# A gated linear attention with a mixture of experts: the state's part of the outputs on four array quarters, a new order on TensorE, decays in three buffers with a budget, and choices for six chunks at a time

## The chip, the cores and the metric

The kernel runs on one core of a Trainium2 chip. The core has a matrix engine (TensorE, PE in the profile; its weight loads are PEld), a vector engine (VectorE, DVE), a scalar engine (ScalarE, ACT), GpSimd (POOL), and SyncE (SP), which issues most of the transfers (DMA). Each engine runs its own list of instructions in order and waits at semaphores for the others. SBUF is the working memory of 128 partitions. PSUM is the memory that TensorE writes to; it has eight banks of 512 float32 numbers per partition.

The metric is the time of one execution on the device in microseconds (us), as the median of several runs.

## What is computed

The reference runs a gated linear attention and gives its result to a mixture of 16 experts in 4 groups:

```python
def _attn_ref(q, k, v, alpha):            # (B, H, S, D) = (4, 8, 768, 48)
    for t in range(S):
        state = alpha[:, :, t, :, None] * state + einsum('bhd,bhe->bhde', k[:, :, t], v[:, :, t])
        y[:, :, t] = einsum('bhd,bhde->bhe', q[:, :, t], state)

def _moe_ref(x, w_group, w_expert, w1, w2):   # x: 3072 tokens of 384
    g_idx = argmax(x @ w_group)               # one of 4 groups, with its softmax weight
    e_idx = argmax(x @ w_expert[g_idx])       # one of 4 experts of the group, with its weight
    out = g_w * e_w * (relu(x @ w1[g, e]) @ w2[g, e])     # 384 -> 1024 -> 384
```

All data are float32. Every token goes to one expert.

## The kernel before

**The attention loop.** The sequence of each of the 4 batches is cut into 6 chunks of 128 tokens. The loop `for n in range(LAST)` (L559) goes over all 24 chunks. The 8 heads are held as 4 pairs (HP = 4). Of a pair, one head lies in partitions 0 to 47 and the other in 64 to 111, so that TensorE can work on both halves of its rows at once. For each chunk there is

- `decayed` (L251): for each pair, two scans on VectorE (L271, L279) that multiply up the decays alpha, backwards and forwards, with a small reciprocal between them (L277), and two products on GpSimd that scale the keys (kp, L274) and the queries (qp, L281). This is done for a *unit* of chunks at once: units have 1, 2 and 3 chunks in batch 0, and 3 and 3 in the others, nine units in all.
- `scores` (L285): for each head, keys times queries on TensorE (L293), 8 matmuls of 128 columns.
- `masked` (L297): the scores go from PSUM to SBUF through an ACT copy (L305) and a GpSimd select that zeroes the future (L306). For some halves VectorE multiplies with a mask instead (L302).
- `turned_keys` (L311): 4 transposes of the keys on TensorE (L318) and an ACT copy (L319).
- `gains` (L322): keys times values, what the chunk adds to the state (L330). `grown` (L336) adds it to the old state on VectorE (L338), and `scaled` (L341) multiplies by the chunk's decay in four ACT instructions (L346). At the end of a batch there is no state to carry, and gains, transposes and state's part are left out.
- `from_before` (L350): the state's part of the chunk's output, state times queries, 8 small products of 48 rows and 48 columns (L358).
- `outputs` (L363): the chunk's own part, values times masked scores (L370), added in PSUM onto the state's part. Each pair's two heads go to the two halves of the output partitions.
- `copied` (L375): an ACT copy of the output to SBUF, named yt.
- `to_rows` (L380): TensorE turns yt into rows by token and multiplies by the group and expert weights in one go (L389). ACT copies the rows to xr (L400), and VectorE sums up the logits (L394).

In a step, TensorE runs: turned keys of n, state's part of n, gains of n, outputs of n, scores of n+1, then to_rows of n.

**The choice.** `choose` (L404) finds group and expert for some chunks at a time with small VectorE instructions (L418 to L435, the picks) and then their weights (L442 to L452). `send` (L455) counts tokens per expert with two matmuls (L462, L463), and VectorE makes a place for every token (L469 to L481). `scatter` writes a chunk's rows to their places in DRAM (slots_d) with an indirect DMA on GpSimd (L490). The choice is made for three chunks at a time (in the last batch three, two and one). Its pieces wait in a queue, `gates`, and the decays' pieces in another, `decays`; `take` (L511) issues a fixed number of them at fixed points of a step.

**What sets the order.** The program is written in the order in which each engine runs it (`manual_schedule`). Only the waits between engines are derived. A pool of PSUM tiles, `bank()`, has seven buffers, one bank each; an eighth bank holds constants.

**Loads.** SP issues the loads of a unit's data (L242, four transfers per unit), the values (L248), a fill of the slots with blanks (L614), and then the expert weights (L178, L180). The first three units are loaded into the buffers that will later hold expert weights, others into seven buffers of their own.

**The experts.** After the loop, 17 jobs run: the first expert's first 128 tokens from the first three batches (`early_rows`, read by L497 once chunk 17 has been scattered), its other tokens, and then one job for each of the other 15 experts, the fullest first. A job has 48 weight tiles, in `hidden` (L639) and `result` (L655). Results go out through VectorE and an indirect DMA on GpSimd (L693). The order of the experts, the rows of the second job (L820) and the weights of the third wait for the last chunk's scatter.

Of the kernel before, what the change touches and what calls it, by code (L numbers as in the profile page):

```python
# [16 lines left out]
ALU = mybir.AluOpType  # L17
# [17 lines left out]
def gla_then_hierarchical_moe(  # L35
# [68 lines left out]
    pp = ctx.enter_context(tc.tile_pool(name="psum", bufs=7, space=PSUM))  # L104
    dp = ctx.enter_context(tc.tile_pool(name="dram", bufs=1, space=DRAM))

    def bank():
        return pp.tile([P, 512], F32, name="bank")
# [55 lines left out]

    early_rows = cp.tile([P, EARLY // 32, QW], F32, name="early_rows")

    weights = {}

    def busy(k, w=P):

        z = bank()
        for _ in range(k):
            nc.tensor.matmul(z[:, 0:w], lhsT=ident, rhs=ident[:, 0:w], start=True, stop=True)
# [29 lines left out]

    with ExitStack() as gla:
        buf = gla.enter_context(tc.tile_pool(name="buf", bufs=1))
        inp = gla.enter_context(tc.tile_pool(name="inp", bufs=7))
        prep = gla.enter_context(tc.tile_pool(name="prep", bufs=2))
        work = gla.enter_context(tc.tile_pool(name="work", bufs=2))
# [6 lines left out]
        NU = len(units)  # L215
        where = {b * NC + c0 + c: (u, c) for u, (b, c0, k) in enumerate(units) for c in range(k)}
# [3 lines left out]
        homes = {}  # L220
        spare, width = [], 0
        for u in range(3):
            w = units[u][2] * (2 * P + A1) + 1
            for p in range(HP):
                if not spare or width + w > DC * F:
                    k = len(spare)
                    spare.append(wp.tile([P, DC, F], F32, name="w1").rearrange("p c f -> p (c f)")
                                 if k % 2 == 0 else
                                 wp.tile([P, FC, DM], F32, name="w2").rearrange("p c f -> p (c f)"))
                    width = 0  # L230
                homes[u, p] = spare[-1][:, width:width + w]
                width += w

        def load(u):
            b, c0, k = units[u]
            at = sum(k_ * (2 * P + A1) + 1 for b_, c_, k_ in units if b_ == b and c_ < c0)
            w = k * (2 * P + A1) + 1
            for p in range(HP):
                t = homes.pop((u, p), None)
                if t is None:  # L240
                    t = inp.tile([P, UC * (2 * P + A1) + 1], F32, name="qka")
                nc.sync.dma_start(out=t[:, 0:w], in_=qka_d[b, p, :, at:at + w])  # L242
                loaded[u, p] = t[0:R]

        def load_v(b, c0=0, c1=NC):
            if c0 == 0:
                vs[b] = prep.tile([P, NC, DM], F32, name="v")
            nc.sync.dma_start(out=vs[b][:, c0:c1].rearrange("p c e -> p (c e)"),  # L248
                                in_=v_d[b, :, c0 * DM:c1 * DM])

        def decayed(u, p):  # L251
# [16 lines left out]
            cq = prep.tile([R, UC, A1], F32, name="cq")[:, 0:k_, :]  # L268
# [14 lines left out]
            return [(1.0, back), (1.2, forth)]  # L283

        def scores(n):  # L285
            u, c = where[n]
            qp, kp, _ = ready[u]
            z = [bank() for _ in heads]
            for p in range(HP):
                if p and n < 2:  # L290
                    busy(1, 64)
                for i, r in enumerate(heads):
                    nc.tensor.matmul(z[i][:, p * P:(p + 1) * P], lhsT=kp[r, p, c, :],  # L293
                                     rhs=qp[r, p, c, :], start=True, stop=True)
            return [t.rearrange("p (h i) -> p h i", h=HP) for t in z]

        def masked(z, on_vector=0):  # L297

            sm = work.tile([P, 2, HP, P], F32, name="sm")
            for i in range(2):  # L300
                if i < on_vector:
                    nc.vector.tensor_tensor(out=sm[:, i], in0=z[i], in1=causal[:, None, :]  # L302
                                            .to_broadcast([P, HP, P]), op=ALU.mult)
                    continue
                nc.scalar.copy(out=sm[:, i], in_=z[i])  # L305
# [5 lines left out]
        def turned_keys(n):  # L311

# [3 lines left out]
            kt = work.tile([P, HP * R], F32, name="kt")  # L316
            for p in range(HP):
                nc.tensor.transpose(zt[:, p * R:(p + 1) * R], kp[:, p, c, :], ident[0:R, 0:R])  # L318
            nc.scalar.copy(out=kt, in_=zt[:, 0:HP * R])  # L319
# [3 lines left out]

# [12 lines left out]
        def grown(n, st, add):  # L336

# [4 lines left out]

# [6 lines left out]

        def from_before(n, st):  # L350
# [3 lines left out]
            z = bank()  # L354
            for p in range(HP):
                for i, r in enumerate(heads):
                    o = slice(64 * i, 64 if i == 0 else R)
                    nc.tensor.matmul(z[o, p * P:(p + 1) * P],  # L358
                                     lhsT=st[r, p, 0:o.stop - o.start], rhs=qp[r, p, c, :],
                                     start=(p == 0), stop=False, skip_group_check=True)  # L360
            return z

        def outputs(n, sm, z):  # L363

            b, bc = divmod(n, NC)
            for p in range(HP):
                for i in range(2):
                    h = 2 * p + i
                    o = slice(64 * i, 64 if i == 0 else R)
                    nc.tensor.matmul(z[o, p * P:(p + 1) * P],  # L370
                                     lhsT=vs[b][:, bc, h * D:h * D + o.stop - o.start],
                                     rhs=sm[:, i, p, :], start=(p == 0 and bc == 0), stop=True,
                                     skip_group_check=True)

        def copied(z):  # L375
            yt = work.tile([R, HP, P], F32, name="yt")
            nc.scalar.copy(out=yt.rearrange("r p s -> r (p s)"), in_=z[0:R, :])  # L377
            return yt

        def to_rows(n, yt):  # L380

# [3 lines left out]
            x, lg = xs[b]  # L385
# [5 lines left out]
            z = z[:, 0:HP * W].rearrange("s (p w) -> s p w", p=HP)  # L391

            def logits():
                nc.vector.tensor_reduce(out=lg[:, bc, :],  # L394
                                        in_=z[:, :, D2:W].rearrange("s p w -> s w p"),
                                        axis=AX.X, op=ALU.add)

            if n + 1 == LAST:
                logits()
# [577 lines left out]
```

## Time and profile before

| | us |
|---|---|
| median of three runs | 430.98 |
| lowest and highest | 430.56, 432.88 |
| the profiled execution | 431.07 |
| its span, first to last instruction | 429.3 |
| first scores on TensorE (L293) | from 6.41 |
| last to_rows of the loop (L389) | 148.55 to 149.70 |
| first expert matmul (L639) | from 151.33 |
| last expert matmul done | 405.6 |
| busy in the span: TensorE, VectorE, ACT, GpSimd | 396.3, 163.8, 124.4, 213.4 |
| busy from 11 to 150: TensorE, VectorE, ACT, GpSimd | 127.3, 98.1, 75.9, 99.6 |
| mean clock granted to TensorE | 0.962 |

A line of a timeline has the start, the duration of the group, the engine, the line of the source, the operation, what it writes and reads, the shapes, how many instructions are merged into the line, and in brackets how long the engine sat idle before it and what ended that. A float32 matmul is recorded as two instructions, so 8 matmuls make x16. The ends of matmuls are modelled, and consecutive groups overlap by some 0.07 us; the time of a group is therefore read from its start to the next one's start.

### The profile page before, as it was taken

How to read it: one execution, taken by the hardware profiler on the slowest of the kernel's cores; microseconds unless marked ns; L12 is line 12 of the kernel's file. 1: busy time of each engine (PE TensorE's matmuls, PEld its weight loads, DVE VectorE, ACT ScalarE, POOL GpSimd, SP SyncE). 2: the span in 40 equal slices, each digit the busy share in tenths (PEclk: the TensorE clock that was granted, in tenths of full speed). 3: DMA queues.
4: the chain of work that ended last, by engine and by line, in shares of the span. 5: the costliest groups of instructions: out<-in, count | busy, mean ns of one | idle time of the engine just before them, and what ended most of it. 6: DMA issues, size and time to landing. Idle time of an engine off the chain costs nothing.

```text
span 429.3 us, 8796 instructions
## 1 busy us (share of the span) xinstructions
PE 396.3 (92%) x3352; PEld 376.9 (88%) x3352; DVE 163.8 (38%) x457; ACT 124.4 (29%) x304; POOL 213.4 (50%) x275
## 2 busy tenths in 40 slices
PE   4998989989889898799999999999999999999991
PEld 3887878778778688799999999999999999999990
DVE  6767668588784471202074120220220222022100
ACT  1466546266465421011121111111111121121110
POOL 7787548597794562210532623623623532452351
PEclk9999889699999989889999999999999999999997
DMA  7998994889111336895865966766876876856000
GB/s 258 394 404 305 359 395 136 263 308 351 53 40 58 96 111 227 223 332 212 274 192 186 279 226 193 245 256 200 241 266 202 271 247 221 300 187 276 34 24 26
DMA packets 32220, 95.23 MB, mean 222 GB/s; under 512 B 18111, under 2 KB 18902, under 8 KB 27696
## 3 DMA queue, kind: packets, MB, share of 16 engines
q1 hardware_dynamic: 27360, 85.10, 58.1%
q0 software_dynamic: 4816, 9.55, 6.8%
q8 instruction: 27, 0.44, 0.4%
q14 instruction: 17, 0.14, 0.1%
HBM read 79.47 MB, written 15.56 MB: 221 GB/s over the span
## 4 chain that ended last, share of the span: by engine, by line
PE 55%; issue 3%; POOL 2%; DMA 1%; DVE 0%; SPq 0%; POOLq 0%; ACT 0%; DVEq 0%; ACTq 0%
PE bank L639 28%; PE bank L655 27%; POOL out_dram L693 1%; DMA slots_d<-xr,place 1%; DMA xq<-slots_d 0%; POOL out_dram L678 0%; POOL yT L628 0%; SPq L820 0%; DVE yq L686 0%; DVE yq L689 0%; POOLq L885 0%; ACT yT L657 0%; DVE dst_q L710 0%; DVE xt_e L701 0%; POOLq L678 0%
## 5 line engine op out<-in xcount | busy, mean ns | idle before, releaser
L693 POOL DMA_INDIRECT out_dram<-yq,dst_q x99 | 96.4, 974 | 158.8 <-DVE yq L689 120.1
L639 PE MATMUL bank<-xt_e,w 128*128 128x128 f32 (+16 forms) x816 | 136.8, 329 | 6.0 <-issue 4.1
L639 PEld LDWEIGHTS bank<-xt_e,w 128*128 128x128 f32 x816 | 133.7, 196 | 6.9 <-issue 6.5
L655 PE MATMUL bank<-hT,w 128*128 128x128 f32 (+16 forms) x816 | 131.8, 321 | 0.0
L655 PEld LDWEIGHTS bank<-hT,w 128*128 128x128 f32 x816 | 129.6, 190 | 0.0
L641 ACT ACTIVATE hT<-bank 128x256 f32<-128x256 f32 (+16 forms) x68 | 32.6, 479 | 108.1 <-PE bank L639 105.7
L710 DVE CAST dst_q<-xq 128x7 int32<-128x7 f32 (+2 forms) x16 | 2.7, 166 | 160.0 <-DMA out_dram<-yq,dst_q 160.0
L657 ACT COPY yT<-bank 128x192 f32<-128x192 f32 (+32 forms) x34 | 13.3, 391 | 113.8 <-PE bank L655 113.8
L306 POOL TENSOR_SCALAR_AFFINE_SELECT sm<-sm 128x512 f32<-128x512 f32 x43 | 26.4, 635 | 27.8 <-ACT sm L305 27.8
L293 PE MATMUL bank<-qp,kp 48*128 48x128 f32 x384 | 31.6, 300 | 6.7 <-POOL qp L281 6.7
L293 PEld LDWEIGHTS bank<-qp,kp 48*128 48x128 f32 x384 | 25.2, 196 | 11.2 <-POOL qp L281 6.9
L370 PE MATMUL bank<-sm,v 128*48 128x128 f32 (+1 forms) x384 | 31.4, 297 | 0.4
L389 PE MATMUL bank<-wr,yt 112*128 112x116 f32 x192 | 28.3, 292 | 1.4 <-ACT yt L377 1.1
L490 POOL DMA_INDIRECT slots_d<-xr,place x24 | 24.2, 1010 | 9.9 <-DVE starts L418 4.7
L305 ACT COPY sm<-bank 128x512 f32<-128x512 f32 x43 | 23.3, 588 | 15.6 <-PE bank L293 14.0
L389 PEld LDWEIGHTS bank<-wr,yt 112*128 112x128 f32 x192 | 24.0, 197 | 3.9 <-ACT yt L377 2.8
L370 PEld LDWEIGHTS bank<-sm,v 128*48 128x48 f32 (+1 forms) x384 | 24.8, 142 | 2.6 <-POOL sm L306 1.2
L358 PE MATMUL bank<-qp,state 48*48 48x128 f32 (+1 forms) x320 | 24.9, 302 | 0.0
L279 DVE TENSOR_TENSOR_SCAN cq<-qka,starts 112x387 f32<-112x387 f32 x24 | 23.0, 959 | 2.5
L346 ACT ACTIVATE state<-gained,rev 112x48 f32<-112x48 f32 x64 | 16.2, 323 | 26.1 <-DVE gained L338 21.9
L281 POOL TENSOR_TENSOR qp<-qka,cq 112x384 f32<-112x384 f32 x24 | 21.9, 914 | 2.6 <-DVE cq L279 2.4
L274 POOL TENSOR_TENSOR kp<-qka,rev 112x384 f32<-112x384 f32 x24 | 22.4, 934 | 1.1 <-DVE rev L271 0.9
(122 smaller groups left out, 300.7 us busy)
## 6 DMA issues: line engine op xcount, KB each, us to landing
w<-in_w_dram SPq DMA_DIRECT2D x32, 1536.0 KB, 7.0
qka<-in_qka_dram SPq DMA_DIRECT2D x24, 578.0 KB, 11.0
slots_d<-blank SPq DMA_DIRECT2D x1, 5488.0 KB, 22.9
v<-in_v_dram SPq DMA_DIRECT2D x3, 1152.0 KB, 14.2
xq<-slots_d SPq DMA_DIRECT2D x32, 85.8 KB, 7.3
w<-in_qka_dram SPq DMA_DIRECT2D x4, 578.0 KB, 9.5
xq<-slots_d SPq DMA_DIRECT2D x28, 73.5 KB, 6.1
out_dram<-yq,dst_q POOLq DMA_INDIRECT x99, 5.8
```

The source lines that it names most:

```text
L279: nc.vector.tensor_tensor_scan(out=flat(cq), data0=a[:, 0:W], data1=st, initial=1.0, op0=ALU.mult, op1=ALU.min)
L293: nc.tensor.matmul(z[i][:, p * P:(p + 1) * P], lhsT=kp[r, p, c, :], rhs=qp[r, p, c, :], start=True, stop=True)
L305: nc.scalar.copy(out=sm[:, i], in_=z[i])
L306: nc.gpsimd.affine_select(out=sm[:, i], in_=sm[:, i], pattern=[[0, HP], [1, P]], compare_op=ALU.is_ge, fill=0.0, base=0, channel_multiplie ...
L358: nc.tensor.matmul(z[o, p * P:(p + 1) * P], lhsT=st[r, p, 0:o.stop - o.start], rhs=qp[r, p, c, :], start=(p == 0), stop=False, skip_group_ ...
L370: nc.tensor.matmul(z[o, p * P:(p + 1) * P], lhsT=vs[b][:, bc, h * D:h * D + o.stop - o.start], rhs=sm[:, i, p, :], start=(p == 0 and bc == ...
L389: nc.tensor.matmul(z[:, p * W:(p + 1) * W], lhsT=yt[:, p, :], rhs=wr[:, p, :], start=True, stop=True)
L490: nc.gpsimd.indirect_dma_start(out=slots_by[t], out_offset=bass.IndirectOffsetOnAxis(ap=place[:, c:c + 1], axis=0), in_=x[:, c0 + c, :], i ...
L639: nc.tensor.matmul(z[:, k * n:(k + 1) * n], lhsT=w1[:, dc, f * P:(f + 1) * P], rhs=xt[:, dc, 0:n], start=(dc == 0), stop=(dc == DC - 1))
L641: nc.scalar.activation(out=hT[:, f0:f0 + 2, 0:n], in_=z[:, 0:2 * n].rearrange("p (f t) -> p f t", f=2), func=AF.Relu)
L655: nc.tensor.matmul(z[:, i * n:(i + 1) * n], lhsT=w2[:, f, dc * P:(dc + 1) * P], rhs=hT[:, f, 0:n], start=(f == 0), stop=(f == FC - 1))
L693: nc.gpsimd.indirect_dma_start(out=out_by.popleft().rearrange("n (j w) -> (n j) w", j=4), out_offset=bass.IndirectOffsetOnAxis(ap=dst[:, b ...
```

## The change

1. `from_before` and `outputs` write a PSUM tile of two banks, pair p into bank p % 2. `side` gives the half of the output partitions: for odd pairs the two heads change sides. So the 8 small products of the state's part lie on all four combinations of row half and column half. On the host, the rows of `wr` are swapped for the even pairs to match. `copied` reads both banks.
2. TensorE's order in a step is now: outputs of n, gains of n, scores of n+1, turned keys of n+1, to_rows of n, state's part of n+1. PSUM has three single banks, one tile of two banks for the scores, and one of two for the outputs. The tiles sm, kt and yt have one buffer instead of two.
3. The decays have three buffers (qp, kp, rev) instead of two. They are issued by `decay`, which is given a budget in us at two points of a step. The loads go in turn into twelve fixed places, and a unit's load is issued when the unit three before has been issued.
4. The choice is made once per batch for six chunks in batches 0 and 1, for three and three in batch 2, and for three, two and one in batch 3. The picks come one step after the last chunk, the counts, weights and places in the step after that. VectorE masks one half of the scores in every step in which no part of a choice is due.
5. The filler matmuls `busy` are gone. The first expert's early rows are turned ahead of the last step. The fill with blanks is issued after step 5 instead of step 2.

```diff
-        inp = gla.enter_context(tc.tile_pool(name="inp", bufs=7))
-        prep = gla.enter_context(tc.tile_pool(name="prep", bufs=2))
-        work = gla.enter_context(tc.tile_pool(name="work", bufs=2))
+        inp = gla.enter_context(tc.tile_pool(name="inp", bufs=1))
+        prep = gla.enter_context(tc.tile_pool(name="prep", bufs=3))
+        work = gla.enter_context(tc.tile_pool(name="work", bufs=1))
+        banks["of"] = gla.enter_context(tc.tile_pool(name="psum_a", bufs=3, space=PSUM))
+        pairs = gla.enter_context(tc.tile_pool(name="psum_b", bufs=1, space=PSUM))
...
-            return [(1.0, back), (1.2, forth)]
+            return [(0.13 + 0.27 * k_, back), (0.31 + 0.27 * k_, forth)]
+        def side(p, i):
+            c = (i + p + 1) % 2
+            return slice(64 * c, 64 if c == 0 else R)
...
+        def of(z, p):
+            return z[:, p % 2, p // 2 * P:(p // 2 + 1) * P]
...
-            z = bank()
+            z = pairs.tile([P, 2, 512], F32, name="zo")
             for p in range(HP):
                 for i, r in enumerate(heads):
-                    o = slice(64 * i, 64 if i == 0 else R)
-                    nc.tensor.matmul(z[o, p * P:(p + 1) * P],
-                                     lhsT=st[r, p, 0:o.stop - o.start], rhs=qp[r, p, c, :],
-                                     start=(p == 0), stop=False, skip_group_check=True)
+                    o = side(p, i)
+                    nc.tensor.matmul(of(z, p)[o], lhsT=st[r, p, 0:o.stop - o.start],
+                                     rhs=qp[r, p, c, :], start=(p < 2), stop=False,
+                                     skip_group_check=True)
...
+        def gate(kind):
+            if kind == "picks":
+                choices.append(choose(*complete.popleft()))
+                next(choices[-1])
+                powers.pop()()
+                next(choices[-1])
+            elif kind == "counts":
+                sendings.append(send(*chosen.pop(0)))
+                next(sendings[-1])
+            elif kind == "weights":
+                next(choices.popleft(), None)
+            else:
+                for _ in sendings.popleft():
+                    pass
+        cuts = {b: (NC,) if b < B - 2 else (UC, NC) if b < B - 1 else (UC, NC - 1, NC)
+                for b in range(B)}
...
+        def decay(us, until=-1):
+            budget[0] += us
+            while made[0] < NU or todo:
+                u = todo[0][0] if todo else made[0]
+                if u > until and budget[0] <= 0 or u > until + 1:
+                    break
+                if not todo:
+                    for p in range(HP):
+                        todo.extend((u, *of_) for of_ in decayed(u, p))
+                    made[0] += 1
+                u, cost, fn = todo.popleft()
+                fn()
+                budget[0] -= cost
+                if not todo and u + 3 < NU:
+                    load(u + 3)
+            budget[0] = min(budget[0], 0.0)
...
+        decay(0, 0)
+        zs = scores(0)
+        kt = kept(turned_keys(0))
+        sm, st, z, last_z = masked(zs, 1), None, None, None
+        decay(0, 1)
...
+            z = outputs(n, sm, z)
+            yt = copied(z)
+            if carry:
+                sums = grown(st, gains(n, kt))
+                st = scaled(n + 1, sums)
+            if more:
+                zs = scores(n + 1)
+                sm = masked(zs, 0 if due else 1)
+                scatter()
+                if n > EARLY_T - 2:
+                    scatter()
+                decay(1.5)
+                if (n + 2) % NC and n + 2 < LAST:
+                    kt = kept(turned_keys(n + 1))
+                if "counts" in due:
+                    gate("counts")
+            zr = to_rows(n, yt)
+            nc.scalar.copy(out=quarters[:, n, :, 0:D2], in_=zr[:, :, 0:D2])
+            logits(n, zr)
+            if bc + 1 in cuts[b]:
...
+                tasks[n + 1] = ("picks",) + tasks.get(n + 1, ())
+                tasks[n + 2] = ("counts", "weights", "places")
+            if carry:
+                z = from_before(n + 1, st)
...
+            if more:
+                spent = 0.0
+                for kind in due:
+                    if kind != "counts":
+                        gate(kind)
+                        spent += 2.1 if kind == "picks" else 1.1
+                decay(1.7 - spent, where[min(n + 2, LAST - 1)][0])
```

`where[n]` gives the unit of chunk n; `due` is the list of the choice's parts for this step, taken from `tasks`.

## The prediction

> **What bounds the kernel now.** I read the page's slices first, then the chain of waits, then TensorE's timeline in the attention loop, then the list of who waited for whom, then the clock by stretches. The chain starts at 157.60 us: from there on it is expert matmuls almost without a gap, and the change does not touch them. So the question is when the loop over 24 chunks ends; its last to_rows (L389) ends at 149.70. TensorE's rows there give the price of each group, from start to next start:
>
> ```profile
> 100.95 1.08 PE L358 MATMUL bank<-qp,state 48*64 48x128 f32 x16
> 101.96 0.61 PE L330 MATMUL bank<-v,kt 128*64 128x48 f32 x15
> 102.47 1.05 PE L370 MATMUL bank<-sm,v 128*64 128x128 f32 x15
> 103.45 1.16 PE L293 MATMUL bank<-qp,kp 48*128 48x128 f32 x16
> 104.69 1.15 PE L389 MATMUL bank<-wr,yt 112*128 112x116 f32 x8
> 105.67 0.55 PE L318 MATMUL bank<-ident,kp 112*128 112x112 f32 x4
> 106.15 1.08 PE L358 MATMUL bank<-qp,state 48*64 48x128 f32 x16
> ```
>
> State's part (L358) 1.01, gains (L330) 0.51, outputs (L370) 0.98, to_rows (L389) 0.98 to 0.99, turned keys (L318) 0.48. Scores (L293) take 1.09 where nothing is waited for (49.89 to 50.98); here TensorE waits some 0.15 for yt behind them. A step without waits is thus 5.06. What is lost beside this:
>
> ```profile
> 76.17 0.20 PE L462 MATMUL bank<-picked,before 128*128 128x48 bf16 x1 [1.54 <-DVE picked L435]
> 76.23 2.03 PE L389 MATMUL bank<-wr,yt 112*128 112x116 f32 x8
> 78.19 1.97 PE L358 MATMUL bank<-qp,state 48*64 48x128 f32 x16
> ```
>
> ```profile
> PE bank L462 <- DVE picked L435: 9.3, 6, 1.5
> ```
>
> ```profile
> 76.23:83.58 7.35, 7.35 (x58) 6.36 (x59) 3.09 (x14) 1.07 (x2) 3.08 (x4) 0.54 0.78 230
> ```
>
> Six times the choice's matmul waits 1.5 us for VectorE (9.3 in all), and after four of these the clock falls: groups take 1.9 to 2.0 instead of 1.0. The last line (stretch, busy times, granted clock 0.54) covers the worst, which costs some 3.4 us; the stretches from 41.79, 57.71 and 126.35, at 0.64, 0.69 and 0.69, cost about 1.7 each. So the loop gives away 9.3 + 8.5 us.
>
> VectorE and GpSimd make the decays. One head of a three-chunk unit:
>
> ```profile
> 16.00 0.94 DVE L271 TENSOR_TENSOR_SCAN rev<-w,starts 112x387 f32<-112x387 f32 x1
> 16.97 0.18 DVE L277 RECIPROCAL starts<-rev 112x3 f32<-112x3 f32 x1
> 17.26 0.96 DVE L279 TENSOR_TENSOR_SCAN cq<-w,starts 112x387 f32<-112x387 f32 x1
> 18.13 0.93 DVE L271 TENSOR_TENSOR_SCAN rev<-w,starts 112x387 f32<-112x387 f32 x1
> ...
> 41.98 0.91 POOL L281 TENSOR_TENSOR qp<-qka,cq 112x384 f32<-112x384 f32 x1 [0.19 <-DVE cq L279]
> ```
>
> A head takes 2.14 us of VectorE (16.00 to 18.13; 2.15 in the next stretch), the second scan ends 2.22 after the first starts, and GpSimd's product ends 0.09 + 0.91 later. Before, these heads are issued one or two pieces at a time, a unit ahead.
>
> **The change, part by part.** *The budget.* decay(1.5) in mid-step has until=-1, and its break on u > until + 1 then holds for every unit but 0: it issues nothing. decay(1.7 - spent, unit of chunk n+2) ignores the budget for a unit that is due. A unit of 8 pieces costs 8.24, which leaves the budget at about -6.5; two steps at 3.2 do not refill it, and in the third the next unit is due whole. The order of instructions says the same: for units 2 to 8 all twelve VectorE instructions of a unit stand in one row at the end of steps 1, 4, 7, 10, 13, 16 and 19, behind that step's logits and choice work, and the eight GpSimd products stand so too. The scores of step n+1, for chunk n+2, need this very unit, and to_rows of n+1 is queued behind them.
>
> The price of one block, counted from the issue end of to_rows(n) on TensorE: ACT's copy and the logits end 0.96 later (134.03 against 134.75 + 0.24). Then any weights-and-places work G, then three heads at 2.14, then 2.22 + 0.09 + 0.91 for the last, then 0.05 to TensorE: 0.96 + G + 9.70. TensorE meanwhile has state's part 0.55 (below), outputs 0.98, gains 0.51 and three of four score pairs, 0.82: 2.86, or 2.35 at a batch's end without gains. So the last pair waits 7.8 + G four times (steps 2, 8, 14, 20) and 8.3 + G three times (5, 11, 17): 56.1. G is 2.14 for three chunks (L442 at 97.78 to the last L469's end at 99.92), at steps 16 and 19; for six chunks, at steps 7 and 13, three more counts at 0.16 and wider rows make 2.9: 10.1 in all. At steps 7, 13 and 19 a second ACT copy of the scores comes ahead of the logits' copy, 0.5 each: 1.5. Waits: 67.7 us. Late behind the block on VectorE is also the growing of the state (0.35, then 1.01 on ACT); it is done some 10.0 after the block starts, ahead of TensorE's need, so it adds nothing.
>
> *The clock after a wait.* TensorE has little to do for 8 to 11 us, then runs dense. Rows: after 1.5 us of idling the clock cost 0, 1.7 or 3.4 us; after the 2.5 us idle before 179.40 the next 48 matmuls take 11.99 instead of the 8.64 of the following job, 3.4 lost. I take 2.6 per block, between 1.7 and 3.4: 18.2, ends 11.9 and 23.8. The Trainium skill, "TensorE: Matmul & The Clock Gate", section "Why this matters for your kernels", says to leave no gap over about 3 us between bursts, since one idle window halves the clock; a window of 3.4 us there, at half rate, would make 7 x 1.7 = 11.9 of the 18.2. It speaks against this change, and the rows at 76.23 show that a shorter gap can already cost twice that.
>
> *Four quarters.* State's part now puts its eight small products on both row halves and both column halves, into two banks. No row shows four at once. Nearest: gains issue the same 16 instructions in 0.51, on two halves and with 48 columns; L358 itself takes 1.01. I take 0.55, nearer to gains, as half of 1.01 is 0.505; ends 0.51 and 1.01. A loss is excluded as far as shapes go, since a step has the same four kinds of group before and after. The Trainium skill, "TensorEngine Tiling (Array Packing)", section "Key Properties", says that a change of tiling mode drains the array; the trace shows each group's start 0.07 ahead of the last one's modelled end, so no drain beyond the prices above, and I add none.
>
> *The order.* Picks are made a step ahead of their counts, so the six waits of 1.54 and what follows them go. Scores' mask now needs: gains' issue end + 0.21, growing 0.35, scaling 1.01 (to +1.67), ACT copy 0.59, GpSimd 0.64: +3.05; TensorE gets to outputs at 1.09 + 0.48 + 0.99 + 0.55 = +3.11. It fits, barely; if not, outputs wait. With two copies on ACT the second half is ready at +3.65, and outputs need it at +3.6. The 0.69 that VectorE now spends on one half lies in its idle time outside the blocks.
>
> *TensorE's work* from step 1's to_rows (issue end 24.22 before) to step 23's: 19 state's parts x 0.55, 22 outputs x 0.98, 18 gains x 0.51, 21 scores x 1.09, 17 turned keys x 0.48, 22 to_rows x 0.99 = 94.0, and 0.8 for yt in the last step: 94.8.
>
> *Start and end.* Unit 1's block stands behind VectorE's mask of chunk 0 and ends some 0.8 after the time before; the filler matmuls go, so the clock may rise later than before, where gains at 14.77 are the first group at its full speed: 2.0. Together +2.8, ends 0 and 4. The first expert's rows are turned before the last step, but the last picks now come some 6.0 after to_rows(23) (4.5 before), while the last scatter, behind fewer others on GpSimd, comes at +8.3 instead of 159.04 - 149.53 = 9.5: -1.2, ends -3.3 and +2. The chain goes through that scatter and SP's fetch. The blank fill and the loads, three units ahead on SP, have 10 us and more in hand, as four loads take 5.7 us (landings at 24.29 to 28.58).
>
> **Sum.** 24.22 + 2.8 + 94.8 + 67.7 + 18.2 = 207.7 for to_rows(23), against 149.53: +58.2. With -1.2, the span goes from 429.3 to 486.3. The profiled execution took 431.07, 1.77 more than its span (the median is 430.98): 488.
>
> **Rivals.** *Faster: TensorE never waits for the decays.* The loop is then TensorE's 94.8: 24.22 + 2.8 + 94.8 = 121.8, -27.7, and with -1.2: 402. For it speaks that VectorE is busy for only 86.80 of the 125.30 us of 24.4 to 149.7. Against it: its queue is in order, and the blocks stand behind logits that TensorE itself releases. It decides where a block costs less than 28.9 / 7 = 4.1 us, waiting and clock together; I have 12.3.
>
> *Slower, but less: cheaper blocks.* If GpSimd's two products set a head's pace, 0.93 + 0.91 = 1.84 instead of 2.14, seven blocks give back 8, and if the score pairs that trickle through keep the clock up, 18: 462. Against it: VectorE's own three rows fill the 2.14.
>
> *Slower still: no gain from the quarters (+8.7) and two slow windows after every block (+5.6):* 502. For it: the worst wait in the trace did cost 3.4.
>
> **Chances.** Forecast 0.80, faster rival 0.04, cheaper blocks 0.08, slower still 0.08. The likeliest gives 488. All low ends together are 476, all high ones 507; with some of the cheaper case I give 474 to 504. Within 0.5% is about what a measurement of this kernel can't tell from no change: 0.01; faster by more 0.04, slower by more 0.95.
>
> **What would show it.** Right: seven waits of 8 to 11 us ahead of the scores, ended by GpSimd's qp; twelve VectorE decay instructions in a row; a clock near 0.5 behind them; state's part at about 0.55; no wait at the counts in the loop. Wrong: these waits under 4 us, or decays between other work; then 402 is nearer. If state's part stays at 1.0, the time goes to 497.

## The result, and the profile after

The changed kernel takes 492.44 us (median of four runs, 491.96 to 494.03), the kernel before 431.93 beside it (four runs, 430.56 to 434.98). The ratio is 1.140, with a 95% interval of 1.133 to 1.147. The profiled execution has a span of 490.5 us and a mean granted clock of 0.900 (0.962 before). Where an execution ran over 1.5% longer than the fastest of its kernel, the ratios below leave it out.

The page after: busy time per engine, the clock's slices, and the shares of the chain that ended last.

```profile
PE 407.9 (83%) x3332; PEld 383.2 (78%) x3332; DVE 165.7 (34%) x434; ACT 119.9 (24%) x293; POOL 208.2 (42%) x262
...
PEclk9987878696959596779999999999999999999997
...
PE 66%; DVE 19%; ACT 4%; issue 4%; POOL 3%; DMA 1%; SPq 0%; POOLq 0%; DVEq 0%; ACTq 0%
```

The low digits of the clock fill the first half of the span, where the attention loop is, and VectorE now holds 19% of the chain, where it had 0% before. TensorE's busy time is no guide: it has fewer instructions (3332 against 3352) and is still busy longer (407.9 us against 396.3), because the mean clock of the loop is down to 0.77.

TensorE's timeline in a step between two blocks of decays:

```profile
97.48 1.06 PE L384 MATMUL bank<-wr,yt 112*128 112x116 f32 x8
98.47 0.66 PE L353 MATMUL zo<-qp,state 48*48 48x128 f32 x16
99.07 1.09 PE L365 MATMUL zo<-sm,v 128*48 128x128 f32 x16
99.98 0.63 PE L322 MATMUL bank<-v,kt 128*48 128x48 f32 x16
100.54 1.16 PE L285 MATMUL zs<-qp,kp 48*128 48x128 f32 x16
```

From start to start, state's part takes 0.60 where it took 1.01, and outputs take 0.91. One step later comes a block; TensorE's timeline again:

```profile
103.30 1.22 PE L365 MATMUL zo<-sm,v 128*48 128x128 f32 x16
106.89 0.49 PE L285 MATMUL zs<-qp,kp 48*128 48x128 f32 x4 [2.36 <-POOL qp L270]
108.96 0.80 PE L285 MATMUL zs<-qp,kp 48*128 48x128 f32 x4 [1.57 <-POOL qp L270]
111.09 0.80 PE L285 MATMUL zs<-qp,kp 48*128 48x128 f32 x4 [1.33 <-POOL qp L270]
113.22 0.80 PE L285 MATMUL zs<-qp,kp 48*128 48x128 f32 x4 [1.33 <-POOL qp L270]
113.94 1.01 PE L307 MATMUL bank<-ident,kp 112*128 112x112 f32 x4
114.74 1.92 PE L384 MATMUL bank<-wr,yt 112*128 112x116 f32 x8
```

The four pairs of the scores start 2.07 to 2.13 us apart, the pace of one head on VectorE, and each waits for a product on GpSimd. From the second pair on the groups take nearly twice their time (0.80 for 0.49, 1.01 for 0.55, 1.92 for 1.06): the clock has fallen. VectorE's timeline in the same 10 us:

```profile
103.53 0.24 DVE L390 TENSOR_REDUCE lg<-bank 128x20 f32<-128x80 f32 x1 [1.03 <-ACT xr L586]
103.69 0.95 DVE L260 TENSOR_TENSOR_SCAN rev<-qka,starts 112x387 f32<-112x387 f32 x1
...
105.77 0.94 DVE L260 TENSOR_TENSOR_SCAN rev<-qka,starts 112x387 f32<-112x387 f32 x1
...
107.84 0.93 DVE L260 TENSOR_TENSOR_SCAN rev<-qka,starts 112x387 f32<-112x387 f32 x1
...
109.97 0.93 DVE L260 TENSOR_TENSOR_SCAN rev<-qka,starts 112x387 f32<-112x387 f32 x1
```

Behind the logits the four heads of the unit stand in one row, nothing between them. Over the loop, the waits of TensorE add up to (engine, line, releaser: total, times, longest):

```profile
PE zs L285 <- POOL qp L270: 63.8, 34, 6.4
PE bank L384 <- ACT yt L373: 3.5, 1, 3.5
PE zo L365 <- POOL sm L297: 1.6, 4, 0.8
```

Of the 63.8 us, 6.4 lie ahead of the first scores of all. The waits for the picks (9.3 us before) are gone from the loop. The last to_rows now ends at 215.5, against 149.7.

The second line is new and belongs to the last step. There, on ACT:

```profile
213.30 0.24 ACT L411 ACTIVATE dl<-dl 128x40 f32<-128x40 f32 x1 [3.83 <-DVE dl L410]
213.44 0.57 ACT L373 COPY yt<-zo 112x512 f32<-112x512 f32 x1
```

and on TensorE:

```profile
209.36 1.24 PE L365 MATMUL zo<-sm,v 128*48 128x128 f32 x16 [0.21 <-POOL sm L297]
214.06 1.45 PE L384 MATMUL bank<-wr,yt 112*128 112x116 f32 x8 [3.46 <-ACT yt L373]
```

The exponential of the picks stands ahead of yt's copy in ACT's order. It waits for VectorE, which has the weights, the places, a transpose of the early rows and the picks to do. So yt, whose matmuls end at 210.6, is copied only at 213.44, and to_rows waits 3.46 us.

### The profile page after: what moved, and what is told of

Same layout as the page of the kernel before. It is cut to its first block, busy times and chain, and to the rows that moved or that the text cites. A ratio compares the mean times of both kernels' runs of the same rounds, so it can differ in the third digit from the quotient of the medians.

```text
span 490.5 us, 8733 instructions
## 1 busy us (share of the span) xinstructions
PE 407.9 (83%) x3332; PEld 383.2 (78%) x3332; DVE 165.7 (34%) x434; ACT 119.9 (24%) x293; POOL 208.2 (42%) x262
## 4 chain that ended last, share of the span: by engine, by line
PE 66%; DVE 19%; ACT 4%; issue 4%; POOL 3%; DMA 1%; SPq 0%; POOLq 0%; DVEq 0%; ACTq 0%
PE bank L634 25%; PE bank L650 25%; DVE cq L268 6%; DVE rev L260 6%; PE zs L285 4%; PE bank L384 4%; PE zo L365 4%; PE bank L307 2%; ACT sm L296 2%; POOL qp L270 2%; PE zo L353 1%; DVE starts L266 1%; PE bank L322 1%; ACT state L338 1%; ACT xr L586 1%
## 5 line engine op out<-in xcount | busy, mean ns | idle before, releaser
L634 PE MATMUL bank<-xt_e,w 128*128 128x96 f32 (+15 forms) x768 | 126.3, 324 | 0.3 <-PE bank L650 0.3
L634 PEld LDWEIGHTS bank<-xt_e,w 128*128 128x128 f32 x768 | 124.1, 190 | 0.5 <-PE bank L650 0.5
L285 PE MATMUL zs<-qp,kp 48*128 48x128 f32 x384 | 45.1, 359 | 63.8 <-POOL qp L270 63.8
L285 PEld LDWEIGHTS zs<-qp,kp 48*128 48x128 f32 x384 | 32.2, 229 | 73.3 <-POOL qp L270 72.2
L365 PE MATMUL zo<-sm,v 128*48 128x128 f32 (+1 forms) x384 | 34.6, 330 | 1.7 <-POOL sm L297 1.6
L365 PEld LDWEIGHTS zo<-sm,v 128*48 128x48 f32 (+1 forms) x384 | 26.3, 158 | 8.8 <-POOL sm L297 4.5
L296 ACT COPY sm<-zs 128x512 f32<-128x512 f32 x34 | 18.7, 580 | 42.9 <-DVE sm L293 41.7
L263 POOL TENSOR_TENSOR kp<-w,rev 112x384 f32<-112x384 f32 (+2 forms) x24 | 19.4, 807 | 10.1 <-DVE rev L260 10.1
L270 POOL TENSOR_TENSOR qp<-w,cq 112x384 f32<-112x384 f32 (+2 forms) x24 | 18.8, 781 | 6.3 <-DVE cq L268 6.1
L373 ACT COPY yt<-zo 112x512 f32<-112x512 f32 x24 | 14.0, 585 | 28.6 <-PE zo L365 27.1
```

What stands on the lines that cost most here:

```text
L270: nc.gpsimd.tensor_tensor(out=qp, in0=q, in1=cq[:, :, 1:A1], op=ALU.mult)
L285: nc.tensor.matmul(z[:, i, p, :], lhsT=kp[r, p, c, :], rhs=qp[r, p, c, :], start=True, stop=True)
L296: nc.scalar.copy(out=sm[:, i], in_=z[:, i])
L365: nc.tensor.matmul(of(z, p)[o], lhsT=vs[b][:, bc, h * D:h * D + o.stop - o.start], rhs=sm[:, i, p, :], start=(p < 2 and bc == 0), stop=Tru ...
L634: nc.tensor.matmul(z[:, k * n:(k + 1) * n], lhsT=w1[:, dc, f * P:(f + 1) * P], rhs=xt[:, dc, 0:n], start=(dc == 0), stop=(dc == DC - 1))
```

## The experiments

No edit below changes what the kernel computes; the results of the added filler matmuls are read by nobody. Medians are compared with runs of the kernel before on the same chip (medians from 430.5 to 432.6).

**1. The blocks spread out.** The two causes of a block are removed together: in mid-step pieces of the next units may be issued too, and the debt left by a unit is limited to 1 us, about one piece.

```diff
-            budget[0] = min(budget[0], 0.0)
+            budget[0] = max(min(budget[0], 0.0), -1.0)
...
-                decay(1.5)
+                decay(1.5, where[n + 1][0])
```

> The changed kernel with two words of the budget altered: the mid-step call may go one unit past the unit of chunk n+1 (until is that unit instead of -1), and the debt is not carried below -1 us. Same instructions, only the decays' pieces stand singly or in pairs between other work instead of in blocks of eight. Theory (TensorE waits because a whole unit stands in one row on VectorE): the waits ahead of the scores fall from 63.8 us to under 15, the loop is paced by VectorE at some 5 us a step, and the time is near 420, between 410 and 435. Rival 1 (it is VectorE's amount of work, not its place): 475 or more, as the work is the same. Rival 2 (the new order on TensorE, the single buffers or the quarters cost the time): still near 492.

Measured: 447.89 us (446.87 to 450.37), ratio 1.037 (1.030 to 1.045). TensorE's waits for the decays:

```profile
PE zs L285 <- POOL qp L270: 31.0, 17, 6.4
```

Half the waits went, and 44.6 us of time with them: more than the 32.8 us of waits, since the clock fell less too (0.86 in the loop, against 0.77). But it is not the 420 expected. The second `decay` of a step gives `1.7 - spent`, so a step with choice work still issues next to nothing, and the unit is then late as a whole. That was the next edit.

**2. No deduction for choice work**, on top of experiment 1:

```diff
-                decay(1.7 - spent, where[min(n + 2, LAST - 1)][0])
+                decay(1.7, where[min(n + 2, LAST - 1)][0])
```

> The run with spread decays (447.9), and in addition the end-of-step budget is not cut by the choice's cost, so that no more than one head of a unit is left to the last moment in most units. Theory: the waits for qp ahead of the scores fall from 31 us to under 16, fewer low-clock stretches follow, and the time is 426, between 415 and 438. Rival (VectorE's amount of work is the bound by now): 443 or more.

Measured: 435.34 us (433.94 to 437.51), ratio 1.014 (1.005 to 1.023). Waits for the decays are 11.9 us, 6.4 of them at the start. So three versions have 63.8, 31.0 and 11.9 us of these waits and take 492.4, 447.9 and 435.3 us: the time falls by 1.36 us per us of wait between the first two and by 0.66 between the last two. The last figure is below 1 because other waits take their place: those for masks grow from 2.1 to 7.3 us, and 2.5 us for the state come up.

**3. The last step's picks behind yt's copy**, on top of experiment 2:

```diff
             if not more:
...
-                for kind in due:
-                    gate(kind)
             z = outputs(n, sm, z)
             yt = copied(z)
+            if not more:
+                for kind in due:
+                    gate(kind)
```

> The run before this one, and in the last step the picks and their ACT exponential are issued behind outputs and yt's copy instead of ahead of them. Theory (to_rows of the last chunk waits 3.1 to 3.5 us for yt, which stands on ACT behind the exponential, which waits for VectorE): some 2 to 3 us less than the run without this. Rival (the picks, and so the last scatter, come later by as much): no difference.

Measured: 431.74 us (429.40 to 433.50, ten runs), ratio 1.005 (1.000 to 1.009), 3.6 us less than without the edit. The wait for yt in the last step goes from 3.4 to 0.75 us:

```profile
154.22 1.15 PE L384 MATMUL bank<-wr,yt 112*128 112x116 f32 x8 [0.75 <-ACT yt L373]
```

The step itself gets 2.9 us shorter in the traces, so most of the 3.6 is this wait; the medians' spread (433.94 to 437.51 without the edit) covers the rest. This is as far as the new order came in these runs: level with the kernel before, not faster, although no wait in mid-loop is longer than 1.6 us. TensorE's waits up to its last to_rows:

```profile
PE zs L285 <- POOL qp L270: 11.9, 9, 6.4
PE zo L365 <- POOL sm L297: 8.7, 14, 1.6
PE zo L353 <- ACT state L338: 2.5, 2, 1.5
```

The decays, spread over the steps, are now ahead of the masks and of the state's growing on VectorE, and outputs and state's part wait for these. Its loop from the second to_rows to the last takes 127.8 us at a clock of 0.93; the kernel before takes 125.3 for the same stretch.

**4. Wide filler matmuls in the blocks**, on the changed kernel. They go into the time in which TensorE waits, so the block's waits should stay and only the clock be kept up.

```diff
+            first = {3: 2, 6: 2, 9: 5, 12: 2, 15: 5, 18: 4, 21: 4}.get(n, 0)
+            if first:
+                spare_z = bank()
             for p in range(HP):
+                for w in () if not first else (512,) * first if p == 0 else (512, 256):
+                    nc.tensor.matmul(spare_z[:, 0:w], lhsT=ident, rhs=blank[:, 0:w],
+                                     start=True, stop=True)
```

> As the run with fillers, but with wide ones (512 and 256 columns per weight load instead of 64), since with the narrow ones the clock fell as before: two to five ahead of the first pair of scores, 768 columns between the pairs. Their results are read by nobody. Theory (a low clock behind a block costs some 3 us a block, and it falls because the array streams little): the clock stays up through the blocks, and the time falls from 492 to about 471, between 465 and 479. Rival (fillers hold up the scores, or the clock falls whatever TensorE is given): 488 or more.

Measured: 472.22 us (471.30 to 473.88), ratio 1.099 (1.090 to 1.108). 20.2 us less than the change, with the blocks all there. One of these steps, from to_rows to to_rows, with the fillers (L288) and the pairs of scores between:

```profile
48.41 1.15 PE L390 MATMUL bank<-wr,yt 112*128 112x116 f32 x8
...
53.67 0.49 PE L291 MATMUL zs<-qp,kp 48*128 48x128 f32 x4 [0.46 <-POOL qp L270]
54.09 1.56 PE L288 MATMUL bank<-blank,ident 128*128 128x512 f32 x4
55.74 0.49 PE L291 MATMUL zs<-qp,kp 48*128 48x128 f32 x4
...
60.86 1.06 PE L390 MATMUL bank<-wr,yt 112*128 112x116 f32 x8
```

The steps that hold a block take 12.4 us (the three without choice work) and 14.8 to 16.0, the steps behind them 4.4 to 4.6; without the fillers they take 13.9 to 14.0 and 16.3 to 17.5, and 5.2 to 6.0. Added up over the steps, from the second to_rows to the last but one, the clock cost 20.0 us: 11.4 inside the block steps and 8.6 behind them.

**5. Narrow filler matmuls in the same places**, 64 columns instead of 512, 126 of them instead of 66:

```diff
+                for _ in range((first if p == 0 else 3) if first else 0):
+                    nc.tensor.matmul(spare_z[:, 0:64], lhsT=ident, rhs=ident[:, 0:64],
+                                     start=True, stop=True)
```

> The changed kernel with filler matmuls on TensorE in the seven waits (5 to 13 small ones ahead of the first pair of scores, 3 ahead of each other pair), whose results nobody reads. Theory (the low clock behind a block costs some 3 us a block, apart from the wait): the waits end where they did, the groups behind them run at full speed, and the time falls by 7 x 3 = 21 to about 471, between 466 and 478. Rival (the groups behind a block are slow for another reason, or the fillers hold up the scores): 488 or more.

Measured: 492.28 us (491.62 to 493.40), ratio 1.138 (1.131 to 1.146): no gain at all, a miss. The loop's stretch, with busy times of TensorE, its weight loads, VectorE, ACT and GpSimd, and then the granted clock; first with the narrow fillers:

```profile
27.00:216.00 189.00, 169.99 (x1791) 148.42 (x1791) 93.86 (x244) 65.77 (x172) 89.88 (x108) 0.77 0.42 146
```

and with the wide ones:

```profile
27.00:195.00 168.00, 156.31 (x1670) 109.38 (x1668) 94.08 (x242) 64.57 (x172) 89.12 (x107) 1.00 0.46 163
```

TensorE is recorded busy for 90% of the first stretch and 93% of the second, yet the clock is 0.77 in one and 1.00 in the other. The weight loads tell them apart: 79% of the first stretch against 65%. But so do the gaps: the narrow fillers left waits for qp of up to 2.3 us (14.6 in all), the wide ones of 0.8 at most (6.8 in all). The next run was made to part the two.

**6. Narrow fillers without gaps**: as 5, with 8 to 21 of them ahead of the first pair and 6 between pairs.

```diff
-            first = {3: 5, 6: 6, 9: 13, 12: 6, 15: 13, 18: 10, 21: 10}.get(n, 0)
+            first = {3: 8, 6: 9, 9: 21, 12: 9, 15: 21, 18: 18, 21: 18}.get(n, 0)
...
-                for _ in range((first if p == 0 else 3) if first else 0):
+                for _ in range((first if p == 0 else 6) if first else 0):
```

> The narrow fillers of 64 columns left waits of 0.8 to 2.3 us ahead of the pairs; the wide ones 0.2 to 0.8. Here there are enough narrow ones to fill these at full clock: 8 to 21 ahead of the first pair instead of 5 to 13, and 6 between pairs instead of 3 (three took 0.88 us and left 0.76 at full clock). If idle gaps decide the clock, it now stays up, the scores in the blocks take 0.49, and the time is about 472 us (467 to 479), as with wide fillers. If it is the data streamed behind each weight load that counts, the clock falls in the blocks all the same; a filler then takes some 0.51 us, six of them 3.1, and with the pair's 0.8 the pairs come 3.9 us apart instead of 2.1, so a block grows by up to 5.3 us, seven by up to 37: 505 to 530 us. Anything near 492 would leave it open.

Measured: 503.16 us (496.78 to 505.62), ratio 1.154 (1.143 to 1.165). Every run is slower than the change's longest (494.03), as the streaming theory has it, but the time is at the low end of its range or below it. The profile below is of a run of 505.35 us; the kernel's mean clock was low in all four runs (0.906 to 0.937, against 0.981 to 0.988 in those of experiment 4). TensorE's loop with them, and a block from its first pair on:

```profile
27.00:222.00 195.00, 190.37 (x1987) 169.98 (x1986) 91.15 (x229) 64.14 (x170) 88.56 (x106) 0.81 0.40 140
```

```profile
86.98 0.49 PE L291 MATMUL zs<-qp,kp 48*128 48x128 f32 x4 [0.48 <-POOL qp L270]
87.40 2.08 PE L288 MATMUL bank<-ident 128*128 128x64 f32 x12
89.41 0.80 PE L291 MATMUL zs<-qp,kp 48*128 48x128 f32 x4
90.14 2.82 PE L288 MATMUL bank<-ident 128*128 128x64 f32 x12
92.89 0.80 PE L291 MATMUL zs<-qp,kp 48*128 48x128 f32 x4
```

TensorE is busy for 98% of the loop, waits for qp 2.8 us in all and never longer than 0.5, and the clock still falls in every block: six fillers go from 1.55 us to 2.82 and the pair from 0.49 to 0.80. It falls up to three pairs later than with the gaps. So filling the gaps is not enough to hold the clock; what the array streams behind each weight load makes the difference (weight loads fill 87% of this stretch). The wide fillers also read other data (zeros, for most of them), so that width alone does it is likely but not shown.

**7. The changed kernel without the quarters**: the heads of every pair stay on their halves.

```diff
-            c = (i + p + 1) % 2
+            c = i
...
-    wx[0::2] = wx[0::2, ::-1].copy()
```

> The changed kernel with the state's part on two diagonal quarters as before (both heads of a pair keep their side; the host's swap is undone), still in two banks. Theory (four quarters work at once and save 0.42 us in each of 20 state's parts, more where the clock is low): state's part back at 1.0, time 500 to 502. Rival (the quarters save nothing where TensorE waits for decays anyway): 492 within 1.

Measured: 503.82 us (502.69 to 505.36), ratio 1.164 (1.156 to 1.172). State's part at full clock takes 1.02 again, from the first row's start to the second's:

```profile
130.43 1.08 PE L353 MATMUL zo<-qp,state 48*64 48x128 f32 x16
131.45 0.80 PE L365 MATMUL zo<-sm,v 128*64 128x128 f32 x6
```

So the quarters give 11.4 us in the changed kernel. At full clock, 20 times 0.42 would be 8.4; five state's parts run at half clock, and there the quarters save twice that (1.06 against 1.90).

**8. The quarters alone, in the kernel before**: `side`, the two-bank tile, `copied` and the rows of `wr` as in the change; five single banks beside the tile of two; order, decays and choice as before.

```diff
-                    o = slice(64 * i, 64 if i == 0 else R)
-                    nc.tensor.matmul(z[o, p * P:(p + 1) * P],
+                    o = side(p, i)
+                    nc.tensor.matmul(of(z, p)[o],
```

> The kernel before with only the state's part on four quarters in two banks (five single banks and one pair instead of seven single). Theory: 20 state's parts at 0.59 instead of 1.01 give back up to 8.4 us, but in six steps TensorE then waits that much longer for VectorE's picks, so 6 us: 425, between 422 and 428. Rival (VectorE sets the pace of the loop before too): 430 or more.

Measured: 427.11 us (424.90 to 428.19), ratio 0.991 (0.987 to 0.994): 4.0 us less, a gain, but half of what 0.42 per step would be. A step's timeline (TensorE, ACT, and TensorE's weight loads):

```profile
63.19 0.66 PE L367 MATMUL zo<-qp,state 48*48 48x128 f32 x16
63.36 0.54 ACT L321 COPY kt<-bank 128x448 f32<-128x448 f32 x1
...
63.94 0.48 PEld L332 LDWEIGHTS bank<-v,kt 128*64 128x64 f32 x15 [0.33 <-ACT kt L321]
```

In the order of before, gains follow state's part and need kt. Its copy ends at 63.90, so gains start 0.75 after state's part, 0.75 or 0.83 in most steps, instead of 1.01; 20 times some 0.2 is near the 4.0. The waits for the picks grew as well, as expected, but only from 9.3 to 10.4 us. In the changed order outputs follow, which find their masks ready in most steps, and the next group starts 0.60 later.

**9. The counts a step later, in the kernel before**: the choice's matmuls are issued ahead of the next step's pieces, when the picks have long been made.

```diff
+            if n < FASTER:
+                send_chosen()
...
-            send_chosen()
+            if n >= FASTER:
+                send_chosen()
```

> The kernel before with only the choice's two counting matmuls moved one step later on TensorE (up to step 20), so that the picks are done when they are reached. Theory (the six waits of 1.5 us and the low clock behind four of them cost 9.3 + 8.5 us): 413, between 410 and 420. Rival (the waits move to another place, as VectorE's work stays the same): 427 or more.

Measured: 419.67 us (417.09 to 420.08), ratio 0.971 (0.966 to 0.976). The picks' waits are gone, and with them the low clock of the loop (two stretches: before, and with this edit):

```profile
24.00:150.00 126.00, 114.32 (x1548) 99.09 (x1546) 87.45 (x266) 68.91 (x180) 88.81 (x113) 0.93 0.63 228
```

```profile
24.00:139.00 115.00, 109.91 (x1551) 94.13 (x1550) 87.25 (x265) 68.62 (x181) 89.36 (x113) 1.00 0.68 248
```

The clock goes from 0.93 to 1.00. 11.5 us came of the 17.8 that the prediction found given away: waits for yt (2.9 us in five) come up, the steps take 5.2 instead of 5.06, some 5.9, and one near the end 6.6.

**10. Both in the kernel before** (8 and 9):

> The two edits to the kernel before together, four quarters and counts one step later. Theory (both gains add up, as the waits for the picks are gone): 431 - 17.8 - 8.4 = 405, between 401 and 412. Rival (VectorE's 86.8 us of work in 125 us, in its order, becomes the bound): 415 or more.

Measured: 417.01 us (416.98 to 421.19), ratio 0.966 (0.963 to 0.970). This is the lowest median of the study, but only 2.7 us below experiment 9, whose runs (417.09 to 420.08) lie within its own: a gain over it is not shown. TensorE's waits in the loop are now:

```profile
PE bank L399 <- ACT yt L386: 3.1, 8, 0.9
PE zo L379 <- POOL sm L308: 2.7, 11, 0.6
PE bank L332 <- ACT kt L321: 1.6, 5, 0.9
```

Where TensorE set the step, the chain through ACT and GpSimd (scores, mask, outputs, yt) seems to set it now; a shorter state's part makes TensorE arrive early and wait. That these waits swallowed the rest is read from this view; no run took them away.

**11 and 12. More fillers at the start.** In the profile of experiment 10 the second to_rows ends at 29.55, 4.8 us later than in experiment 9, since its groups run at half speed until about 26 us. (This is read from their durations, 0.80 for a pair of scores instead of 0.49; the profile's clock figure says 1.00 there.) But that execution took 421.19 us, and the other four, of which there is no trace, 416.98 to 417.08: the late start may be its own. Wider fillers (`busy(1)` for `busy(1, 64)`, and `busy(5)` ahead of the first scores) were tried on experiment 10's kernel and on the kernel before.

```diff
-                    busy(1, 64)
+                    busy(1)
...
+        busy(5)
```

> The kernel before with four quarters and counts one step later (417.0), and with five filler matmuls ahead of the first scores, from the time the identity is ready, and fillers of 128 columns instead of 64 between the first two chunks' scores. Theory (groups run at half speed until about 26 us in that run, since narrow fillers between waits do not bring the clock up): full speed from some 10 to 15 us on, 4 to 6 us less, 412, between 409 and 415. Rival (the start waits for loads and decays, not for TensorE): 416 or more.

> The kernel before with the same fillers at the start alone. Theory (there the clock is up from about 14.8 us, and what is behind waits for decays): 1 to 3 us less, 428 to 430. Rival (no effect, or the fillers delay the first scores): 431 or more.

Measured: 418.11 us (416.93 to 420.32), ratio 0.967 (0.962 to 0.973), and 431.88 (429.03 to 436.05), ratio 0.999 (0.996 to 1.003): misses, no gain in either. On experiment 10's kernel the second to_rows did end at 24.83, but some groups near the loop's end ran at half clock, and the loop ended 2.4 us earlier, not 4.7. On the kernel before, the first to_rows came 1.1 us later. So no gain from fillers at the start is shown, and the late start that they were meant to mend may not have been there in most executions.

## Why the prediction was right

The forecast was 488 us, the measurement 492.4. The place (seven blocks of decays that stand between to_rows and the scores it needs) was right, and the sum was short by 7.6 us at the last to_rows (207.9 with the row's own end, 215.5 measured). That the total is only 4.4 off is in part luck: the way from the loop to the third job got 1.9 us shorter than the sum had it, and that job's first 48 matmuls, which took 11.82 us before (179.40 to 191.22), now take 8.83 (242.11 to 250.94), a gain the sum left out; some 1.5 us were lost again later. The steps of the sum, each against what the profile after shows:

| step of the sum | predicted | measured |
|---|---|---|
| to_rows(1) ends (24.22 + 2.8) | 27.0 | 27.1 |
| block step without choice work and at full clock | 0.96 + 9.70 + 0.27 + 0.48 + 0.99 = 12.4 | 12.4 (experiment 4) |
| choice work in a block step of six chunks, with the second copy | 2.9 + 0.5 = 3.4 | 16.0 - 12.4 = 3.6 (experiment 4) |
| state's part | 0.55 | 0.60 |
| the clock, seven blocks | 18.2 | 20.0 (change against experiment 4) |
| step 23, from to_rows to to_rows | 3.3 | 6.95 |
| from the loop to the third job | -1.2 | -3.1 |

*The waits* held, by the time at which they end: in the block shown, the last pair starts at 113.22, and the prediction's 10.66 us from 102.71 on give 113.37. The recorded idle time is smaller than its 67.7 us (55.6 from 27 us on, 6.6 in that block instead of 8.3), as TensorE's own groups fill more of the wait than it had (0.80 for a pair, not 0.41). In experiment 4, where the clock doesn't blur them, a block step takes the 12.4 us that the prediction had worked out from one head's pace. Experiments 1 and 2 show that the waits cause the loss: as they went, the time went, down to 435. Together with the 3.6 us of the last step, removing them brings the change level with the kernel before.

*The clock's term* was 1.8 us short: 2.86 per block against 2.6, inside the bounds of 1.7 and 3.4. The Trainium skill, "TensorE: Matmul & The Clock Gate", section "Why this matters for your kernels", asks for no idle gap over about 3 us between bursts. Four blocks begin with a gap of 4.4 to 5.3 us, and there the first pair already takes 0.80, in line with it. The gaps in the block shown are 2.4, 1.6, 1.3 and 1.3 us, all shorter, and the clock fell there too; in experiment 6 no wait for the decays was over 0.5 us in the loop, and it fell as well. The measurement decides: keeping gaps short was not enough here.

*The last step* was the mis-sized term of most weight, 3.6 us. The prediction gave it 0.8 for yt, as TensorE's work sets it, and took ACT to be free. It had counted what is queued behind VectorE's blocks, but not that in step 23 the picks' exponential stands ahead of yt's copy on ACT and waits for VectorE. Experiment 3 moved it, and the kernel took 3.6 us less, 2.9 of them in this step. The remaining 2.2 us lie mostly in the steps without a block: 4.73 and 4.24 to 4.28 where 4.6 and 4.12 were worked out, and small differences in the choice work.

*The quarters* were worth what was said or a little more in the changed kernel (11.4 us, experiment 7, against 8.7 for "no gain" in the rival). The Trainium skill, "TensorEngine Tiling (Array Packing)", section "Key Properties", says a change of mode drains the array. The next group starts 0.60 after state's part, with 0.06 of overlap with its modelled end, so no drain shows beside the price of the groups.

*The rivals.* The faster one (402) needed blocks under 4.1 us each. Spreading the decays removed most of their waits and gave 431.7 at best, as other waits, for masks and state, took their place. So in the budgets tried the decays were not hidden in this order; whether another budget would hide them is not shown. "Cheaper blocks" (462) fell: TensorE's few pairs did not keep the clock, and the heads kept VectorE's pace. "Slower still" (502) fell on the quarters, and came close with its second half: 2.86 per block, not 3.4.

*What the kernel before gave away* was found in the right places (experiment 9 took the picks' waits away, and the clock went to 1.00), but of its 17.8 us only 11.5 came back, as other waits came up.

What stays open: what limits the loop of experiment 10 at some 5.1 us per step, where TensorE's own work in a full step is some 4.65 (5.06 less 0.41), and why spread-out decays leave the clock at 0.93.

## What to carry to other kernels

A budget that lets work run "when due, whatever it costs" and then carries the debt forward makes blocks: read the order of instructions that it gives, and price a block from the engine's own rows, as an in-order engine holds up everything that stands behind it. When a stage is moved, look at each engine it issues on, ACT included, and at what stands behind it there in the last step as well as in mid-loop. A local gain (0.42 us in each step here) is worth its full size only where the next group in the engine's order is ready; behind the same eight products, gains that waited for a copy let about half of it through.

## What the runs showed of the hardware

The clock followed what TensorE streamed, not how full its time was with instructions. Fillers of 64 columns left it at 0.81 with TensorE busy for 98% of the loop and no wait for the decays above 0.5 us; fillers of 512 columns (some of 256) held it at 1.00 with 93% and waits of up to 0.8. With the first the kernel took 496.8 to 505.6 us, with the second 471.3 to 473.9, and without fillers 492.0 to 494.0. The two also streamed different data, so the runs don't show that the width alone decides.

Small products of 48 rows and 48 columns took 0.60 us for eight on four array quarters against 1.01 on two halves of the rows, a factor of 1.7.
